# Sixteen query/key projection units moved from the opening stage into the attention rounds of a gated attention-plus-GLU kernel

## The chip, the cores and the metric

The kernel runs on one core of a Trainium2 chip. The metric is the device time of one execution in microseconds (us), lower is better. The engines are TensorE (PE; its weight loads are listed as PEld), VectorE (DVE), ScalarE (ACT), GpSimd (POOL) and SyncE (SP), which here only issues DMAs. POOL and ACT can issue DMAs too.

## The reference

For 2048 tokens of width 448 the program computes two blocks from the same input and mixes them by a gate that depends on the token:

```python
# A: attention, 16 heads of 28
qkv = (x @ wqkv).reshape(B, S, 3, H, 28)          # -> q, k, v
p = softmax(einsum("bhqd,bhkd->bhqk", q, k) * 28 ** -0.5)
a = einsum("bhqk,bhkd->bhqd", p, v) @ wo
# B: gated linear unit, 1792 hidden
gate = x @ W_gate; up = x @ W_up
b = (relu(gate) * up) @ W_down
g = sigmoid((x * gate_w).sum(-1))
out = g * a + (1 - g) * b
```

## The kernel before

**Arithmetic.** Every fp32 operand of a projection is split into a rounded high part and the rest ("low"), and the products that matter are added up. With the width of 448 laid out as three chunks of 128 and one of 64, a projection of one tile takes 11 matmuls (`TERMS`, `NT` = 11). One such group of 11 that fills one PSUM tile of 128x512 is called a unit here.

**Stage 1, the head** (everything ahead of the rounds). Tokens come in four blocks `tb` of 512. Queries and keys together are 896 columns, or `NQ` = 7 column blocks `c` of 128. So there are 28 units `qk(tb, c)` (L424); each result is split into high and low by ACT and DVE and sent by POOL to DRAM (`qk_d`, L435). There are 16 units `vproj(tb, t)` for the values (L442). The first 9 qk units run alone, three more follow, and the rest alternate with the values (`mixed`, L515 to L519). Keys and queries of heads 0, 1 and 2 are loaded back from `qk_d` by SP (`load_k` L164, `load_q` L169) in a layout that stacks the high and low parts on partitions. The first 36 of the row-maximum tiles (`smax`, L190: two matmuls and one DVE reduction) and the first 8 score tiles are mixed into the later units; `first = 9` says from which place of `mixed` on. POOL also writes the split input blocks 1 to 3 to DRAM (`spill_x`, L395), since their room in SBUF is needed.

**Stage 2, 32 rounds.** A round is half a head: 8 of the 16 key blocks against all queries. What each engine does in a round, and in which order, is written out as a string of letters (`ROUNDS`, L46 to L71); the loop at L740 reads it and records the instructions in that order. The letters that matter here:

- `s`: one score tile, two matmuls (L306) and one evacuation by ACT (L310 with the exponential, L312 as a copy); `m`: one maximum tile (L200, L204)
- `x`: one matmul of the gate and up projections (L600). 22 of them, two units, make one hidden block `i`; ACT takes the relu of the gate half (L610), DVE multiplies (L613), SP stores the product
- `w`: split the next gate/up weights into high and low on ACT and POOL (`split_f`, L572)
- `b`, `A`: running minimum over key blocks (L256) and its reduction over partitions on DVE (L263 to L279); `g`: subtract that from 4 tiles on POOL (L285); `e`: exponential of two of the 4 tiles on ACT (L296)
- `P`, `Q`: 32 matmuls each of probabilities times values (L653), 64 a round
- `n`, `N`, `c`, `f`: small steps that end a head; `D`: split a block of W_down; `l`, `u` in the first round finish the last qk unit and load head 2

All engines take their instructions in the written order, and so does SP its DMAs. The rounds hold 1188 `x`, which is 54 of the 56 hidden blocks. The gate itself (`gates`, L553: sigmoid of 16 columns) runs in round 0 through `small_things(1)`.

**Stage 3, the tail.** Two more hidden blocks, the output projection of attention (`wout`), the product with W_down (`down`, L906) and the final mix, in an order written as a list `todo` (L922 to L950).

Of the kernel before, what the change touches and what calls it, by code (L numbers as in the profile page):

```python
# [32 lines left out]
NQ = 2 * D // P  # L33
WARM = 11
# [11 lines left out]
FIRST = "sbbsbAxxxxlusxgxsxxsxssxsxxxsxxsesxxxxbegxxseexwPbbAQ"  # L46

A1 = "smsxxxswbxxxsgbsbnxxxxxssxssxxsAxemxwxmgxsmxxmcessxxxsmxsxbxeggxxxxxesebxeefbewxmmNAwPQ"

Ee = "gswmwsxxxxbsxgsxsxxbebxxxsxxssxxAxssxxemxxxmxsmxeexgmxxsexmxmxxsemxxxsgsbesbbewAwPQ"  # L50

Oe = "sgmgwsxxxxbssxxxsxbxxbxnsxsxsxsAwsxmxxemxxsmxeemsegwxmxxxxmsmxxgexNxsxsbesbxexbcwefxPAQ"

A8 = "wwwsmsxxsxxxxbsxbxgsexxsbxxxxsssxxgxxsAxmxmexxsxemxxgxmsxmexxmsxmxexxgessbbesPewbAQ"

O = "ssbnsxxxxsxbxNxbxxggsxxxxsxxxsxsxxssxxAmxsxxemsxmxexxmxsmxxemmgexsbxxxsbcxxxsbxAxmgeePefeQ"
# [28 lines left out]
def gated_mix_kernel(ctx, tc, x, wq, wo, wgu, wd, out):  # L85
# [49 lines left out]
    x_d = {(tb, r): dram.tile([P, 4 * TB + P], F32, name=f"x_d_{tb}_{r}")[:, :4 * TB].rearrange("p (c t) -> p c t", c=4) for tb in range(1, NB) for r in range(2)}  # L135
# [27 lines left out]

    def load_k(h):  # L164
        k = qk_d[2 * DH * h:2 * DH * h + DH].rearrange("d r t -> (d r) t")
        for a in (0, 2 * DH):
            nc.sync.dma_start(f32(K[h % 3])[a:a + 2 * DH], k)

    def load_q(h):  # L169
        Q[h] = QS[h % 3].rearrange("p j t -> p (j t)")  # L170
        if h > 2:
            nc.sync.dma_start(f32(Q[h])[GD:GD + 2], f32(Q[h])[GD + 2:GD + 4])
        for a in range(2):
            for r in range(2):
                nc.sync.dma_start(f32(Q[h])[2 * DH * a + r:2 * DH * (a + 1):2], qk_d[2 * DH * h + DH:2 * DH * (h + 1), a])
# [112 lines left out]
    def take_exp():  # L288
        q = min(todo_exp, key=lambda q: (q[0], q[2], -q[1]))
        k = halves.pop(q, 0)  # L290
        if k:
            todo_exp.remove(q)
        else:
            halves[q] = 1
        q = QUAD[q][:, 2 * k:2 * k + 2].rearrange("p c t -> p (c t)")
        nc.scalar.activation(q, q, AF.Exp, scale=-SCALE)  # L296
# [35 lines left out]


    with tc.tile_pool(name="qkv", bufs=1) as pa:
        W = pa.tile([P, 7, 2 * D + VC], F32R, name="W")
# [78 lines left out]
        def st_tile(tb, c):  # L414

            k = sent[0]
            sent[0] += 1
            if k < 15 and k % 5 > 2:
                return outs[k % 5 - 3]
            if c == NQ - 1 and tb == 0:  # L420
                return pair[0][:, 2:].bitcast(F32R)
            return pa.tile([P, 2, TB], F32R, name=f"st_{tb}_{c}", tag="st", bufs=3)

        def qk(tb, c, terms=TERMS, among=()):  # L424
            ps = ps_any(f"qk_{tb}_{c}", c == NQ - 1)
# [3 lines left out]
            st = st_tile(tb, c)  # L429

            def send():
                act_high(st[:, 0], ps)
                low(st[:, 1], ps, st[:, 0])
                queue = nc.sync if (tb, c) == (0, NQ - 1) else nc.gpsimd
                queue.dma_start(qk_d[c * P:(c + 1) * P, :, tb * TB:(tb + 1) * TB], f32(st))  # L435


            sends.append(send)
            if (tb, c) != (0, NQ - 1):
                sends.pop()()  # L440

        def vproj(tb, t, among=()):  # L442
            ps = ps_any(f"v_{tb}_{t}", tb == 0 and t > 1)
            for n, (a, b) in enumerate(TERMS):
                nc.tensor.matmul(ps[:, :VC], xf(tb, b)[:, t * P:(t + 1) * P], W[:, a, 2 * D:], start=(n == 0),  # L445
# [46 lines left out]
        w2 = load_w(2)  # L492
# [4 lines left out]
        split_w(*w2)  # L497
# [14 lines left out]
        units = [(qk, 3, 1), (qk, 2, 2), (qk, 3, 2)]  # L512
        units += [(qk, tb, c) for c in range(3, NQ) for tb in range(NB - 1, -1, -1)]
        vs = [(vproj, tb, t) for tb in range(NB - 1, -1, -1) for t in range(4)]
        mixed = units[:2]  # L515
        units = units[2:]
        while units or vs:
            mixed += units[:1] + vs[:1]
            units, vs = units[1:], vs[1:]  # L519
        spills = {15 + 3 * k: (NB - 1 - k // 2, k % 2) for k in range(6)}  # L520
        m, first, ahead = 0, 9, MAXIMA
        for n, (f, *a) in enumerate(mixed):
            if n == 0:
                split_w(*w5)
            if n == 6:
                load_k(1)
                load_q(1)
            if n == 8:
                split_w(*w3)
            if n == 13:  # L530

                nc.gpsimd.memset(f32(K[2])[96:128], -1.0)
            if n == 16:
                load_k(2)
            if n == len(mixed) - 6:
                fetch_f(0)
            if n in spills:
# [23 lines left out]
    fe = ctx.enter_context(tc.tile_pool(name="fe", bufs=1, side="right"))  # L561
# [8 lines left out]
    done = starts[-1] // (2 * NT)  # L570
    assert len(ROUNDS) == 2 * H and starts[-1] % (2 * NT) == 0 and done <= NB * NF, (len(ROUNDS), starts)
# [24 lines left out]

    def gu_mm(ps, i, s, n):

        a, b = (BY_CHUNK if i else HIGH_FIRST)[n]
        nc.tensor.matmul(ps, WS[i][:, s, a], xf(i // NF, b), start=(n == 0), stop=(n == NT - 1))  # L600
# [44 lines left out]
    def pv(v, part):  # L645
# [11 lines left out]
        if v % 2 == 0:  # L657
            OS[h] = fe.tile([P, TB], F32, name=f"os_{h}", tag="os", bufs=2)
# [55 lines left out]
    passes = [(*divmod(k, 2), n) for k in range(2 * done) for n in range(NT)]  # L714
# [3 lines left out]
    def small_things(u):  # L718
# [6 lines left out]
        if u == 1:  # L725
            gates()
# [261 lines left out]
```

## Time and profile before

| quantity | value |
|---|---|
| median of 3 timed runs | 1201.19 us (1199.29 to 1202.57) |
| span of the profiled execution | 1198.9 us |
| PE busy | 1183.7 us, 6183 matmuls |
| DVE, ACT, POOL busy | 902.8, 878.2, 748.9 us |
| head | 0 to 131.3 us |
| rounds 0 to 31 | 131.3 to 1007.4 us |
| tail | 1007.4 to 1198.9 us |

The profiled execution has no time of its own beside its span; the median of the timed runs lies 2.3 us above that span, so much lies around the first and the last instruction or is spread between executions. A round is taken to end when its last probability-times-value matmul has started, and the head when the last value matmul has started. [...]

### The profile page before, as it was taken

How to read it: one execution, taken by the hardware profiler on the slowest of the kernel's cores; microseconds unless marked ns; L12 is line 12 of the kernel's file. 1: busy time of each engine (PE TensorE's matmuls, PEld its weight loads, DVE VectorE, ACT ScalarE, POOL GpSimd, SP SyncE). 2: the span in 40 equal slices, each digit the busy share in tenths (PEclk: the TensorE clock that was granted, in tenths of full speed). 3: DMA queues.
4: the chain of work that ended last, by engine and by line, in shares of the span. 5: the costliest groups of instructions: out<-in, count | busy, mean ns of one | idle time of the engine just before them, and what ended most of it. 6: DMA issues, size and time to landing. Idle time of an engine off the chain costs nothing.

```text
span 1198.9 us, 16948 instructions
## 1 busy us (share of the span) xinstructions
PE 1183.7 (99%) x6183; PEld 820.1 (68%) x6183; DVE 902.8 (75%) x1179; ACT 878.2 (73%) x1082; POOL 748.9 (62%) x326
## 2 busy tenths in 40 slices
PE   9999999999999999999999999999999999999998
PEld 6888755556656666666666666666666666899997
DVE  6466798888898989898888989898988653544242
ACT  5321789999999888888788888888888896422121
POOL 4222387889897777766676767777767786522020
PEclk9999999999999999999999999999999999999999
DMA  9956354354535453443536443436443425743342
GB/s 317 319 207 250 136 191 137 111 141 143 156 129 159 148 163 114 124 122 117 150 119 186 118 129 110 128 117 191 112 126 105 138 89 161 218 136 119 114 128 75
DMA packets 63486, 178.35 MB, mean 149 GB/s; under 512 B 13050, under 2 KB 19650, under 8 KB 58754
## 3 DMA queue, kind: packets, MB, share of 16 engines
q1 hardware_dynamic: 56812, 151.53, 41.1%
q0 software_dynamic: 6160, 25.30, 5.5%
q8 instruction: 48, 0.79, 0.3%
q10 hardware_dynamic: 432, 0.46, 0.1%
q14 instruction: 34, 0.28, 0.1%
HBM read 118.58 MB, written 58.87 MB: 148 GB/s over the span
## 4 chain that ended last, share of the span: by engine, by line
PE 85%; DVE 5%; ACT 3%; DMA 3%; issue 1%; POOL 1%; SPq 1%; DVEq 0%; POOLq 0%; ACTq 0%
PE gu L600 19%; PE s L306 18%; PE po L653 18%; PE sm L200 10%; PE acc L893 10%; PE qk L427 6%; PE wo L852 3%; PE v L445 3%; DVE r L256 1%; ACT P L310 1%; DVE mx L204 1%; ACT P L312 1%; ACT P L296 1%; DMA ls<-os 1%; DMA wor<-wo_d 1%
## 5 line engine op out<-in xcount | busy, mean ns | idle before, releaser
L285 POOL TENSOR_TENSOR P<-P,rm 128x2048 f32<-128x2048 f32 x102 | 470.7, 4633 | 95.5 <-DVE rm L279 79.7
L600 PE MATMUL gu<-X,wg 128*128 128x512 f32 x1232 | 364.6, 395 | 0.7 <-ACT rl L610 0.7
L204 DVE TENSOR_REDUCE mx<-sm 128x1 f32<-128x1024 f32 x256 | 301.5, 1215 | 40.9 <-PE sm L200 40.5
L306 PE MATMUL s<-Q,K 128*128 128x512 f32 x1024 | 316.8, 405 | 6.2 <-ACT V L310 1.9
L600 PEld LDWEIGHTS gu<-X,wg 128*128 128x128 f32 x1232 | 231.2, 188 | 56.7 <-ACT rl L610 2.0
L306 PEld LDWEIGHTS s<-Q,K 128*128 128x128 f32 x1024 | 178.1, 188 | 98.5 <-DVE mn L265 13.4
L312 ACT ACTIVATE P<-s 128x1024 f32<-128x1024 f32 x204 | 202.9, 1031 | 44.2 <-PE s L306 41.6
L653 PE MATMUL po<-P,V 128*32 128x512 f32 x1640 | 227.7, 594 | 0.4 <-ACT P L296 0.4
L296 ACT ACTIVATE P<-P 128x1024 f32<-128x1024 f32 x204 | 213.2, 1072 | 2.1 <-POOL P L285 1.8
L310 ACT ACTIVATE P<-s 128x1024 f32<-128x1024 f32 x206 | 201.5, 1039 | 9.0 <-PE s L306 7.7
L256 DVE SCALAR_TENSOR_TENSOR r<-s,r 128x1024 f32<-128x1024 f32 x124 | 151.6, 1223 | 19.0 <-ACT P L312 10.5
L200 PE MATMUL sm<-K,Q 128*128 128x512 f32 x520 | 163.7, 399 | 0.7 <-DVE mx L204 0.6
L653 PEld LDWEIGHTS po<-P,V 128*32 128x32 f32 x1640 | 63.5, 110 | 116.3 <-issue 108.8
L653 PE MATMUL po<-V 128*32 128x512 f32 x408 | 135.9, 594 | 0.0
L285 POOL TENSOR_TENSOR V<-V,rm 128x2048 f32<-128x2048 f32 x24 | 111.1, 4634 | 23.0 <-DVE rm L279 19.3
L121 ACT ACTIVATE hh<-hr 128x512 fp32r<-128x512 f32 x52 | 32.8, 631 | 117.9 <-PE acc L893 111.8
L200 PEld LDWEIGHTS sm<-K,Q 128*128 128x128 f32 x520 | 91.3, 188 | 33.2 <-ACT P L310 5.6
L127 DVE TENSOR_TENSOR hh<-hr,hh 128x512 fp32r<-128x512 f32 x52 | 47.8, 926 | 82.6 <-ACT hh L121 78.9
L893 PE MATMUL acc<-WD,hh 128*128 128x448 f32 x480 | 100.7, 368 | 0.0
L893 PEld LDWEIGHTS acc<-WD,hh 128*128 128x128 f32 x480 | 90.1, 188 | 8.8
L256 DVE SCALAR_TENSOR_TENSOR r<-s,P 128x1024 f32<-128x1024 f32 x50 | 61.1, 1223 | 38.3 <-ACT P L312 38.3
L271 DVE TRANSPOSE_TENSOR_REDUCE mn<-r 128x32 f32<-128x1024 f32 x63 | 78.0, 1238 | 1.3
(87 smaller groups left out, 1142.6 us busy)
## 6 DMA issues: line engine op xcount, KB each, us to landing
wg<-ws_d SPq DMA_DIRECT2D x42, 896.0 KB
K<-qk_d SPq DMA_DIRECT2D x32, 448.0 KB
Q<-qk_d SPq DMA_DIRECT2D x64, 224.0 KB
h_d<-h SPq DMA_DIRECT2D x56, 256.0 KB
hr<-h_d SPq DMA_DIRECT2D x52, 256.0 KB
ws_d<-wg SPq DMA_DIRECT2D x14, 896.0 KB
qk_d<-st POOLq DMA_DIRECT2D x21, 512.0 KB, 3.2
wgr<-wgu SPq DMA_DIRECT2D x13, 512.0 KB
```

The source lines that it names most:

```text
L200: nc.tensor.matmul(ps[:, c, :], Q[h][:, u * P:(u + 1) * P], K[h % 3][:, k0:k0 + TB], start=True, stop=True)
L204: nc.vector.tensor_reduce(to, ps, axis=AX.XY, op=OP.max)
L256: nc.vector.scalar_tensor_tensor(r, ps, -1.0, before, op0=OP.mult, op1=OP.min)
L271: nc.vector.tensor_reduce(MN[:, 1:3], R2.pop((v, j)).rearrange("p a (b r) -> p a b r", r=32), axis=AX.X, op=OP.min, apply_transpose=True)
L285: nc.gpsimd.tensor_tensor(QUAD[q], QUAD[q], m, op=OP.subtract)
L296: nc.scalar.activation(q, q, AF.Exp, scale=-SCALE)
L306: nc.tensor.matmul(ps[:, c], K[h % 3][:, k * P:(k + 1) * P], Q[h][:, j * TB:(j + 1) * TB], start=True, stop=True)
L310: nc.scalar.activation(dst, ps, AF.Exp, scale=SCALE)
L312: nc.scalar.activation(dst, ps, AF.Copy, scale=-1.0)
L600: nc.tensor.matmul(ps, WS[i][:, s, a], xf(i // NF, b), start=(n == 0), stop=(n == NT - 1))
L653: nc.tensor.matmul(po[32 * j:32 * j + 32], V[:, h // 4 % 2, k, h % 4], AT.pop((v, k, j)), start=(k == k0), stop=(k == k0 + NK // 2 - 1))
L893: nc.tensor.matmul(ACC[i // NF][t][:, :D], HH[i][:, a, t * P:(t + 1) * P], wd_high_low(f, b), start=(f == 0 and n == 0), stop=(f == NF - 1 ...
```

## The change

**Which units move.** Only the column blocks 0, 1 and 2 of queries and keys (`NE` = 3) stay in the head: 12 units, which is all that heads 0 to 4 need. The other four column blocks (`NL` = 4) times four token blocks, 16 units, become the first 176 `x` of the rounds. The gate and up work comes after them in the same stream, so each of its blocks stands 176 `x` later. The strings of letters are new for each round. They hold 1364 `x` in place of 1188, so again 54 hidden blocks are done before the tail. Rounds 0 to 3 hold 44 `x` each (before: 22, 33, 33, 33), rounds 4 to 27 hold 40 or 43 in turn (before 33 up to round 8, then 40 and 37 in turn), the last four 45, 50, 47, 50 (before 37, 47, 41, 44).

```diff
+NE = 3
+NL = NQ - NE
+VO = NE * P
+QP = NL * NB * NT
-E = "gsmsxxxxssebxxbbxxxsxxxxmxAexxssxgsxxsxxsxxmxxsxxemsmexgxexmxxxmsxmxexsbxsgebsebAPQ"
+R12 = "sxxsxxgxxbsxwxbwsbxxxsxxxsxxxssxxAxxswsxgExxmxwmsxxxmxxxsmxsgxxmxxmxxEsbxsgxxsEbebPAmmeQ"
...
+    WB = [fe.tile([P, 7, 2 * P], F32R, name=f"wb_{k}", tag="wg", bufs=2) for k in range(NL // 2)]
...
+    def send_qk(ps, c, tb, queue):
+        high, rest = (fe.tile([P, TB], F32R, name=f"{t}_qk_{c}_{tb}", tag=t, bufs=2) for t in ("rl", "h"))
+        act_high(high, ps)
+        low(rest, ps, high)
+        for r, t in enumerate((high, rest)):
+            queue.dma_start(qk_d[c * P:(c + 1) * P, r, tb * TB:(tb + 1) * TB], f32(t))
...
+    def next_x(tb, n):
+        c = BY_CHUNK[n][1] % 4
+        if n == NT - 1 or BY_CHUNK[n + 1][1] % 4 != c:
+            for r in range(2):
+                nc.sync.dma_start(f32(X[0][r])[:, c], x_d[tb, r][:, c])
+    def qk_mm(ps, u, n):
+        tb, c = divmod(u, NL)
+        a, b = BY_CHUNK[n]
+        nc.tensor.matmul(ps, WB[c // 2][:, a, c % 2 * P:(c % 2 + 1) * P], xf(tb, b), start=(n == 0), stop=(n == NT - 1))
+        if c == NL - 1:
+            next_x((tb + 1) % NB, n)
```

**What goes with it.** The weights of the moved units (`WB`) take the two buffers that the gate/up weights use later; their low parts are made by POOL. The input blocks are needed again in the rounds, so all four of them (8 transfers of 1024 KB in place of 6) go to DRAM, and at the end of each of rounds 0 to 3 the next block is loaded chunk by chunk into the one that is left. The results of the moved units go to DRAM over SP, in two transfers each. In the head every second unit is now sent in two transfers too.

**The head's order.** The three qk units that were followed by qk and v in turn are now followed by the 16 value units alone, and the 36 maximum tiles begin at place 4 of `mixed`:

```diff
-        units = [(qk, 3, 1), (qk, 2, 2), (qk, 3, 2)]
-        units += [(qk, tb, c) for c in range(3, NQ) for tb in range(NB - 1, -1, -1)]
...
-        m, first, ahead = 0, 9, MAXIMA
+        mixed = [(qk, 3, 1), (qk, 2, 2), (qk, 3, 2)]
+        mixed += [(vproj, tb, t) for tb in range(NB - 1, -1, -1) for t in range(4)]
+        spills = {2 + 2 * k: (NB - 1 - k // 2, k % 2) for k in range(2 * NB)}
+        m, first, ahead = 0, 4, MAXIMA
...
-        if u == 1:
-            gates()
...
-    def take_exp():
+    def take_exp(whole):
...
+    before(3, (gates,))
```

On PE, ahead of the first maximum tile (`sm`, which reads the keys `K` and queries `Q` of head 0), there stood before:

```order
L427 MATMUL qk_2_414<-X_3_113,W 128x512 x7
L427 MATMUL qk_2_414<-X_3_114,W 128x512 x4
L445 MATMUL v_0_430<-W,X_3_113 128x450 x7
L445 MATMUL v_0_430<-W,X_3_114 128x450 x4
...
L427 MATMUL qk_3_517<-X_1_117,W 128x512 x7
L427 MATMUL qk_3_517<-X_1_118,W 128x512 x4
L445 MATMUL v_3_532<-W,X_3_113 128x450 x6
L200 MATMUL sm_541<-K_102,Q_105 128x512 x2
```

And at the same place, from the twelfth qk unit to the first maximum tile, there stands now:

```order
L485 MATMUL qk_2_427<-X_3_121,W 128x512 x7
L485 MATMUL qk_2_427<-X_3_122,W 128x512 x4
L500 MATMUL v_0_445<-W,X_3_121 128x450 x7
L500 MATMUL v_0_445<-W,X_3_122 128x450 x4
L500 MATMUL v_1_461<-W,X_3_121 128x450 x4
L255 MATMUL sm_468<-K_104,Q_107 128x512 x2
```

Six units and six matmuls stood between the twelfth qk unit and the first maximum tile; one unit and four matmuls do now.

At the start of round 2, behind the probability-times-value matmuls of round 1, PE had scores (`s`), a maximum tile and the second hidden block's up half (`gu`):

```order
L306 MATMUL s_0_2_1592<-Q_106,K_103 128x512 x2
L200 MATMUL sm_1596<-K_104,Q_1183 128x512 x2
L306 MATMUL s_2_2_1600<-Q_106,K_103 128x512 x2
L600 MATMUL gu_1_1604<-X_111,wg_1284 128x512 x2
L600 MATMUL gu_1_1604<-X_112,wg_1284 128x512
L600 MATMUL gu_1_1604<-X_111,wg_1284 128x512
L306 MATMUL s_4_2_1612<-Q_106,K_103 128x512 x2
L600 MATMUL gu_1_1604<-X_111,wg_1284 128x512
L306 MATMUL s_6_2_1618<-Q_106,K_103 128x512 x2
```

Now the same scores stand there with a projection unit (`qk`, from the weights `wb`) between them:

```order
L361 MATMUL s_0_2_1382<-Q_108,K_105 128x512 x2
L255 MATMUL sm_1386<-K_106,Q_625 128x512 x2
L361 MATMUL s_2_2_1390<-Q_108,K_105 128x512 x2
L669 MATMUL qk_1394<-X_119,wb_113 128x512 x2
L361 MATMUL s_4_2_1398<-Q_108,K_105 128x512 x2
L669 MATMUL qk_1394<-X_120,wb_113 128x512
L669 MATMUL qk_1394<-X_119,wb_113 128x512 x2
L669 MATMUL qk_1394<-X_120,wb_113 128x512
L669 MATMUL qk_1394<-X_119,wb_113 128x512
L361 MATMUL s_6_2_1409<-Q_108,K_105 128x512 x2
```

Between the third and the fourth score tile of the round stand five projection matmuls where one gate/up matmul stood.

**Other edits.** A letter `E` takes the exponential of all four tiles in one instruction where `e` takes two (the other `e` of the pair falls away). `gates` moves from round 0 into the tail, ahead of the fourth `down`. Head 2's keys and queries and the first two gate/up weight blocks are loaded in the head. The packing of column blocks for heads 4 to 15 follows the plain order of the input (`rows_kq`), which changes only row numbers in `qk_d`.

More of the change, by code (lines that the diff above doesn't have):

```diff
@@ L44 @@
 NP = 10
[L46 to L56, printed above, removed]
@@ L133, in gated_mix_kernel @@
     qk_d = dram.tile([2 * D, 2, S + P], F32, name="qk_d")[:, :, :S]
-    x_d = {(tb, r): dram.tile([P, 4 * TB + P], F32, name=f"x_d_{tb}_{r}")[:, :4 * TB].rearrange("p (c t) -> p c t", c=4) for tb in range(1, NB) for r in range(2)}
+    x_d = {(tb, r): dram.tile([P, 4 * TB + P], F32, name=f"x_d_{tb}_{r}")[:, :4 * TB].rearrange("p (c t) -> p c t", c=4) for tb in range(NB) for r in range(2)}
     v_d = {g: dram.tile([P, NK, 4, 32], F32, name=f"v_d_{g}") for g in (2, 3)}
@@ L318, in xf @@
         return X[tb][b // 4][:, b % 4]
-    WR, WS, pair, sends = {}, {}, [], []
+    WR, WS = {}, {}
+    fe = ctx.enter_context(tc.tile_pool(name="fe", bufs=1, side="right"))
+    OX = fe.tile([P, 2, TB], F32, name="ox")
+    WB = [fe.tile([P, 7, 2 * P], F32R, name=f"wb_{k}", tag="wg", bufs=2) for k in range(NL // 2)]
     def fetch_f(i):
@@ L412, in gated_mix_kernel @@
         sent = [0]
[L414 to L422, printed above, removed]
         def qk(tb, c, terms=TERMS, among=()):
-            ps = ps_any(f"qk_{tb}_{c}", c == NQ - 1)
+            ps = ps_any(f"qk_{tb}_{c}")
             for n, (a, b) in enumerate(terms):
@@ L428, in qk @@
                 mix(n, among)
[L429 to L440, printed above, removed]
+            k = sent[0]
+            sent[0] += 1
+            if k % 2:
+                send_qk(ps, c, tb, nc.gpsimd)
+                return
+            st = outs[k // 2 % 2]
+            act_high(st[:, 0], ps)
+            low(st[:, 1], ps, st[:, 0])
+            nc.gpsimd.dma_start(qk_d[c * P:(c + 1) * P, :, tb * TB:(tb + 1) * TB], f32(st))
         def vproj(tb, t, among=()):
@@ L569, in gated_mix_kernel @@
         starts.append(starts[-1] + order.count("x"))
-    done = starts[-1] // (2 * NT)
-    assert len(ROUNDS) == 2 * H and starts[-1] % (2 * NT) == 0 and done <= NB * NF, (len(ROUNDS), starts)
+    done = (starts[-1] - QP) // (2 * NT)
+    assert len(ROUNDS) == 2 * H and (starts[-1] - QP) % (2 * NT) == 0 and done <= NB * NF, (len(ROUNDS), starts)
     def split_f(i, high, low, part=(0, 1)):
@@ L713, in gated_mix_kernel @@
     parts = 0
-    passes = [(*divmod(k, 2), n) for k in range(2 * done) for n in range(NT)]
+    passes = [(*divmod(k, 2), n) for k in range(-NL * NB, 2 * done) for n in range(NT)]
     units = []
@@ L772, in gated_mix_kernel @@
             elif o == "w":
-                ready = -(-starts[v + 2] // NT)
+                ready = -(-max(0, starts[v + 2] - QP) // NT)
                 ready = min(ready + ready % 2, 2 * NF)
-                while parts < ready and (parts < 4 or parts // 2 - 2 in finished):
+                while parts < ready and parts // 2 - 2 in finished:
                     split_f(parts // 2, act_high, pool_low, (parts % 2,))
```

161 lines of the change are left out of this document (95 added, 66 removed).

## The prediction

> **What bounds the kernel now.** I read the page's busy times first, then the chain of work that ended last, then the busy times of each engine by stage.
>
> ```profile
> PE 1183.7 (99%) x6183; PEld 820.1 (68%) x6183; DVE 902.8 (75%) x1179; ACT 878.2 (73%) x1082; POOL 748.9 (62%) x326
> PE 85%; DVE 5%; ACT 3%; DMA 3%; issue 1%; POOL 1%; SPq 1%; DVEq 0%; POOLq 0%; ACTq 0%
> ```
>
> PE is listed as busy nearly all the time and carries 85% of the chain, so work that only changes its place on PE changes nothing by itself. But listed matmuls overlap, and short waits vanish in such a sum. So I price a matmul by the distance between starts, from the timeline of a quiet stretch and from the longest pieces of the chain:
>
> ```profile
> 602.19 1.33 PE L600 MATMUL gu<-X,wg 128*128 128x512 f32 x5
> 603.35 0.64 PE L306 MATMUL s<-Q,K 128*128 128x512 f32 x2
> 592.23 7.00 PE po L653 x64
> ```
>
> Five matmuls in 603.35 - 602.19 = 1.16 us make 0.232 us each; a round's 64 probability-times-value matmuls take 7.00 us. With these two prices I compare need and time by stage (the columns: stretch, length, then busy time and count for PE, PEld, DVE, ACT, POOL, the clock, the DMA share and GB/s):
>
> ```profile
> 0.00:38.30 38.30, 36.47 (x144) 26.12 (x145) 23.64 (x38) 21.00 (x38) 17.28 (x29) 1.00 0.90 312
> 38.30:131.30 93.00, 92.71 (x422) 78.90 (x421) 53.86 (x57) 23.99 (x56) 19.24 (x29) 1.00 0.62 233
> 131.30:186.50 55.20, 51.88 (x277) 30.47 (x275) 49.05 (x60) 49.79 (x66) 40.28 (x23) 1.00 0.48 161
> 186.50:241.70 55.20, 54.29 (x295) 32.98 (x291) 48.39 (x64) 51.45 (x63) 48.16 (x23) 1.00 0.44 136
> 241.70:351.00 109.30, 108.21 (x588) 65.86 (x582) 98.24 (x129) 102.70 (x126) 95.78 (x43) 1.00 0.44 138
> 351.00:377.80 26.80, 26.69 (x149) 16.64 (x145) 23.90 (x30) 24.43 (x28) 20.77 (x7) 1.00 0.56 168
> 377.80:902.90 525.10, 525.08 (x2876) 335.74 (x2871) 465.04 (x618) 459.79 (x519) 382.08 (x119) 1.00 0.45 134
> 902.90:1007.40 104.50, 102.24 (x568) 66.04 (x562) 64.99 (x95) 94.27 (x109) 81.63 (x26) 1.00 0.33 109
> 1007.40:1198.90 191.50, 186.11 (x900) 167.37 (x892) 75.71 (x94) 50.74 (x79) 43.72 (x33) 1.00 0.46 141
> ```
>
> The strings give the matmuls of each stage (one per x, two per s and m). Rounds 4 to 7, the fifth row: 132 + 128 + 64 = 324 at 0.232, and four blocks of 7.00, make 103.2 of 109.3 us, so PE stood 6.1 us. In the same way: rounds 0 and 1 (146 matmuls with what is left of the head) 47.9 of 55.2, 7.3 lost; rounds 2 and 3 51.6, 3.6 lost; round 8 25.8, 1.0 lost; rounds 9 to 27 (1645) 514.6, 10.5 lost, 0.55 a round; rounds 28 to 31 (305) 98.8, 5.7 lost. Together 34.2 us are lost in the rounds. That is all that the rounds can give. Rounds with splits of weights (`w`) and 33 x lose 1.0 to 1.8 each from round 2 on, later ones 0.55. What ends the waits there, in rounds 4 to 7:
>
> ```profile
> PEld s L306 <- ACT P L310: 2.8, 9, 0.6
> PEld s L306 <- DVE mn L265: 2.5, 3, 0.8
> PEld s L306 <- DVE r L256: 2.4, 6, 0.5
> PEld gu L600 <- ACT rl L610: 1.4, 2, 0.7
> ```
>
> PE waits for a PSUM tile that ACT or DVE has not emptied, a few tenths at a time. ACT is busy 102.7 of 109.3 us there, and has the splits to do as well. In the head and the tail PE needs nearly all of the time, while ACT works 24 of 93 us and 51 of 191.5.
>
> **What leaves the head.** The head's timeline on PE:
>
> ```profile
> 1.20 4.10 PE L472 MATMUL warm_ps<-warm 128*128 128x512 bf16 x11 [1.20 <-DVE warm L469]
> ...
> 38.26 2.40 PE L445 MATMUL v<-W,X 128*128 128x450 f32 x11
> 40.50 2.69 PE L427 MATMUL qk<-X,W 128*128 128x512 f32 x11
> 43.03 2.42 PE L445 MATMUL v<-W,X 128*128 128x450 f32 x11
> ...
> 53.83 0.63 PE L200 MATMUL sm<-K,Q 128*128 128x512 f32 x2
> ```
>
> A unit takes 43.03 - 40.50 = 2.53 us, a value matmul (40.50 - 38.26) / 11 = 0.204. Sixteen units fewer: **-40.5 us**.
>
> **What the head gains as a wait.** The first maximum tile stood at 53.83, six units behind the twelfth qk unit. Now it comes after one value unit and four matmuls: 40.50 + 4 x 0.204 = 41.3 us. It needs head 0's keys and queries. When do they land? The queue of SP, its waits from 35 to 60 us, and what the two DMA queues moved from 35.8 to 48.6 us:
>
> ```profile
> 35.87 0.82 SPq L167 DMA_DIRECT2D K<-qk_d  x2
> 36.73 3.38 SPq L175 DMA_DIRECT2D Q<-qk_d  x4
> ...
> 46.20 0.72 SPq L175 DMA_DIRECT2D Q<-qk_d  x1
> SPq L175 <- DMA Q<-qk_d: 0.7, 2, 0.4
> q1 hardware_dynamic: 788, 2.53, 62.1%
> q0 software_dynamic: 401, 1.50, 33.0%
> ```
>
> The loads of head 0 are issued from 35.87 on, and nothing in the change makes that earlier: they wait for the ninth unit's results, as before. The two last issues for head 1 were themselves held until an older query load had landed, the very last one at 46.20; each load of head 0 has a semaphore that a later one uses again. So the second of the four query loads landed at about 46.2, and at about 1.1 us apart (the issue before it stood about that much earlier) the fourth lands at 48.4. The bounds: head 0's six loads are 2 x 448 + 4 x 224 = 1792 KB (1.84 MB); at q1's 2.53 MB in 12.8 us in order of issue they would be there at 35.87 + 9.3 = 45.2; and 53.83 at the latest, since no wait for them is shown. So PE stands from 41.3 to 48.4: **+7.1 us** (3.9 to 12.5). All of PE queues up behind it: the values, then the maxima.
>
> After such a stop PE may also start slowly. The one start from rest that the trace has is the first row above: 11 matmuls of 512 columns from 1.20 to 5.36 (the next start), 0.378 each in place of 0.232, 1.6 us in all. The granted clock is 1.00 in every stage row, so the trace shows no second case. I take **+1.6 us** (0 to 1.6). [...] The 4.10 us row agrees with a slow start; that a pause within a run does it is shown by no trace here.
>
> The other edits of the head cost nothing by this trace: DVE has 36 maxima to reduce in 15 units now, but works 53.86 of 93 us; the eight input copies (1024 KB each) are issued by POOL, busy 19.24 of 93, behind the qk results; the DMA share of 0.62 leaves room.
>
> **What the rounds take in.** 1364 - 1188 = 176 matmuls at 0.232: **+40.8 us** if nothing of it fills a wait. The evacuations come along, and the displaced gate/up work takes its own with it to later rounds. Rows for these, for the exponential and for `gates`:
>
> ```profile
> L127 DVE TENSOR_TENSOR st<-qk,st 128x512 fp32r<-128x512 f32 x21 | 14.3, 683 | 10.7 <-ACT st L121 10.7
> L613 DVE TENSOR_TENSOR h<-gu,rl 128x512 f32<-128x512 f32 x56 | 38.2, 681 | 11.8 <-PE gu L600 5.9 <-ACT rl L610 5.9
> L121 ACT ACTIVATE st<-qk 128x512 fp32r<-128x512 f32 x21 | 12.5, 594 | 34.9 <-PE qk L427 34.9
> L296 ACT ACTIVATE P<-P 128x1024 f32<-128x1024 f32 x204 | 213.2, 1072 | 2.1 <-POOL P L285 1.8
> L130 POOL TENSOR_TENSOR wg<-wgr,wg 128x384 fp32r<-128x384 f32 x26 | 25.8, 1012 | 23.8 <-ACT wg L121 21.9 <-POOL mn L636 1.6
> L556 DVE TENSOR_SCALAR e<-e 128x16 f32<-128x16 f32 x1 | 4.3, 4305 | 0.0
> L558 DVE TENSOR_SCALAR gate<-gate 128x16 f32<-128x16 f32 x1 | 4.3, 4251 | 0.0
> ```
>
> In rounds 0 to 3, 16 units with one DVE step each (16 x 0.683 = 10.9 us) replace 5.5 hidden blocks (5.5 x 0.681 = 3.7), 7.2 us more for DVE; against that `gates` leaves it, 8.6 us of round 0. ACT and POOL are rid of the splits there until round 3. In the tail `gates` lies on a DVE that works 75.71 of 191.5 us: 0 (if it held one `down` back as in round 0, 8.6).
>
> **What the rounds give back.** A round now holds 40 to 44 x. PE's need rises to 28.3 us with 44 x (92 x 0.232 + 7.00) and to 27.4 and 28.1 with 40 and 43, while rounds 4 to 7 took 27.3 with their splits. So the longest engine's need is now PE's, and waits for ACT and DVE, whose work per round hardly grows, have more matmuls standing between them. What stays lost, by my choice between the 0.55 that rounds without splits lose now and what rounds with them lose: rounds 0 and 1 2.8 (from 7.3; `gates` gone, no splits), 2 and 3 1.4 (3.6), 4 to 11 6.0 at 0.75 (8.7: splits stay, spread out), 12 to 27 6.4 at 0.40 (8.8), 28 to 31 3.2 (5.7). Together 19.8 of 34.1, given back: **-14.3 us**. The 57 whole exponentials help: two of 512 cost 2 x 594 ns and one of 1024 1072, a fixed part of about 0.1 us, some 6 us of ACT in all, which is not on the path by itself. Bounds: nothing is given back, or all rounds get to 0.35 (11.2 lost), 23 given back.
>
> Reloading the input at the end of rounds 0 to 3 is costed at nothing: the reload of a chunk starts when three of 11 matmuls of the last unit are done, and the round's 7.00 us block stands before the next unit. Without that cover it would cost some us each time.
>
> Sum: -40.5 + 40.8 + 7.1 + 1.6 - 14.3 = -5.3 on the profiled span, and the same on the median of the runs: 1201.2 - 5.3 = 1195.9, I say **1196**.
>
> **The rivals.**
>
> *The rounds take the units at full price.* The waits listed hang on DVE and ACT steps in a fixed order; if a score tile still comes as early after its predecessor as before, x elsewhere does not shorten the wait, and only `gates` and the whole exponentials give something, about 1. Then 1201.2 + 0.3 + 8.7 - 1 = 1209, slower. For it: rounds 9 to 27 lose 0.55 already with ACT at 459.8 of 525.1, so the waits are not one of capacity. Against it: rounds with fewer x lose three times that. It decides when the rounds give back less than 5.4. Chance 0.20.
>
> *Head and rounds cancel out.* The stop at the first maximum is 7 to 9, the rounds give 6 to 12: 1198 to 1204, about 1201. Chance 0.19.
>
> *The stop is short.* Head 0's loads land at 45.2 (POOL's queue yields to SP's), PE does not slow down, and the rounds lose 0.40 each (12.8, so 21.3 given back): 1201.2 + 0.3 + 3.9 - 21.3 = 1184. For it: q1 had only 62.1% of the engines. Against it: the 46.20 row. Chance 0.21.
>
> My forecast has the other 0.40. That the change doesn't do what it says, with the units waiting in the rounds for the reloaded input, would show as PE waiting for a DMA; it belongs to the first rival.
>
> **How the numbers follow.** A measurement of this kernel tells about 0.3% (3.6 us) from no change. Faster by more: forecast and third rival, 0.61; within: 0.19; slower: 0.20. The range reaches from the third rival's side (1182 with 23 given back and 3.9 lost, and a little beyond, since the 0.35 is my choice: 1180) to 1209.
>
> **What would show it.** Right: the value stage's first maximum at about 48 with PE idle 7 us before it, waiting for a load of Q; the last value matmul near 102 (131.3 less 15 units of 2.53 and plus 8.7: 102.0); rounds 4 to 7 lasting about 28.5 each; the tail as long as before. Wrong: a first maximum that starts at 42; rounds 12 to 27 that lose over 0.6 each; a PE wait for X at the seam of rounds 0 to 3.

## The result, and the profile after

The changed kernel takes 1207.38 us (median of 4 runs, 1206.96 to 1207.83) against 1201.12 us (4 runs, 1199.29 to 1202.57): ratio 1.0062, 95% interval 1.0046 to 1.0078. It is slower by 6.3 us, where 5.3 faster was forecast. The profiled run took 1207.77 us with a span of 1206.0, so 1.8 us lie around it (before: 2.3). That is near enough to compare by spans: 1206.0 - 1198.9 = +7.1 us.

The busy times, the shares of the chain and the granted clock on the page:

```profile
PE 1184.7 (98%) x6183; PEld 825.1 (68%) x6183; DVE 899.1 (75%) x1171; ACT 881.2 (73%) x1023; POOL 746.6 (62%) x325
PEclk9899999999999999999999999999999999999999
PE 86%; DMA 4%; DVE 3%; ACT 3%; issue 1%; SPq 1%; POOL 1%; DVEq 0%; ACTq 0%; POOLq 0%
```

PE does the same 6183 matmuls. ACT has 59 instructions fewer (57 of them by exponentials that were two halves and are one). On the chain DVE fell from 5% to 3% and DMA rose from 3% to 4%. Which DMAs, the list of PE's waits says (total, times, longest):

```profile
PE sm L255 <- DMA Q<-qk_d: 8.1, 1, 8.1
PE gu L661 <- DMA X<-x_d: 3.2, 2, 2.0
PE wo L914 <- POOL on L177: 2.9, 1, 2.9
```

The last of these is old (1.8 us before, and 1.5 to 3.5 in the profiles below: a reason to compare times, and not spans, where 2 us matter). The other two are new. The busy times by stage, cut at the head's end, after rounds 1, 3, 7, 11, 27 and 31:

```profile
0.00:38.30 38.30, 36.79 (x143) 26.80 (x144) 22.31 (x34) 20.15 (x34) 19.19 (x35) 1.00 0.90 304
38.30:105.40 67.10, 59.00 (x263) 50.11 (x262) 43.15 (x38) 18.95 (x45) 14.81 (x24) 0.92 0.77 273
105.40:157.50 52.10, 52.10 (x289) 33.99 (x292) 42.59 (x60) 44.85 (x51) 30.51 (x11) 1.00 0.49 166
157.50:215.70 58.20, 58.20 (x317) 38.00 (x313) 51.77 (x69) 52.16 (x59) 40.87 (x14) 1.00 0.63 204
215.70:330.70 115.00, 114.49 (x623) 72.71 (x615) 98.62 (x128) 105.68 (x122) 100.30 (x48) 1.00 0.52 159
330.70:445.30 114.60, 114.23 (x619) 72.86 (x615) 97.54 (x128) 102.78 (x117) 95.16 (x43) 1.00 0.54 169
445.30:905.80 460.50, 456.89 (x2470) 293.34 (x2466) 400.08 (x526) 390.65 (x416) 320.05 (x98) 1.00 0.44 133
905.80:1014.80 109.00, 108.36 (x591) 68.62 (x585) 65.47 (x96) 95.50 (x102) 81.84 (x27) 1.00 0.36 115
1014.80:1206.00 191.20, 184.61 (x900) 168.62 (x892) 77.55 (x98) 50.50 (x80) 43.88 (x33) 0.99 0.46 142
```

The head ends at 105.4 (131.3 before, 102 forecast), the rounds take 909.4 us (876.1), the tail 191.2 (191.5): -25.9 + 33.3 - 0.3 = +7.1. In the head PE is busy 59.0 of 67.1 us, and the clock column falls to 0.92.

To see the rounds I price every matmul of a round by its start distance in dense stretches of both kernels (0.231 us, and 0.1075 for one of the 64 probability-times-value matmuls) and call the rest of the round lost. These prices are a little lower than the prediction's, so the loss of before is 40.4 us and not 34.2; the differences count.

| rounds | lost before | lost after | given back | forecast |
|---|---|---|---|---|
| 0 to 3 | 11.6 | 2.8 | 8.8 | 6.7 |
| 4 to 11 | 10.6 | 9.5 | 1.1 | 2.7 |
| 12 to 27 | 11.7 | 18.9 | -7.2 | 2.4 |
| 28 to 31 | 6.5 | 5.7 | 0.8 | 2.5 |
| all | 40.4 | 36.9 | 3.5 | 14.3 |

So the first rounds did what was forecast, and rounds 12 to 27 lose more than before. Two of them stand out: round 18 loses 2.5 and round 26 loses 3.8, where most of the others lose about 0.85 (round 25 loses 1.6). The 3.2 us that PE waits for `X` lie in these two.

**The head.** PE's and SP's timelines (start, length, operation, idle time before it):

```profile
38.34 3.23 PE L500 MATMUL v<-W,X 128*128 128x450 f32 x15
49.68 1.19 PE L255 MATMUL sm<-K,Q 128*128 128x512 f32 x2 [8.10 <-DMA Q<-qk_d]
```

```profile
36.37 0.79 SPq L221 DMA_DIRECT2D K<-qk_d  x2
37.20 3.45 SPq L230 DMA_DIRECT2D Q<-qk_d  x4
40.70 1.10 SPq L221 DMA_DIRECT2D K<-qk_d  x2
42.51 4.97 SPq L230 DMA_DIRECT2D Q<-qk_d  x4
48.06 0.61 SPq L403 DMA_DIRECT2D wr<-wq  x1
```

The loads of head 0 are issued where they were, and the first maximum waits for the last of them, from 41.6 to 49.7. The two matmuls of that maximum are then listed at 1.19 us, where the first pair of before took 0.63. The last SP row will matter too: one load of weights of the moved units, issued behind 12 key and query loads of two heads.

**The seams.** The gate/up work goes through the four input blocks in turn, and at three places the next block is loaded over the last one, 8 transfers of 256 KB by SP. Before, these lay in rounds 9, 17 and 25. With 176 matmuls ahead of the stream they lie in rounds 11, 18 and 26. Even rounds also carry the next head's key and query loads on the same queue. SP in round 18, and at the start of round 26:

```profile
629.39 1.71 SPq L742 DMA_DIRECT2D rb<-l_d  x4
631.20 0.84 SPq L656 DMA_DIRECT2D X<-x_d  x2
632.09 0.65 SPq L226 DMA_DIRECT2D Q<-Q  x1
632.79 3.15 SPq L230 DMA_DIRECT2D Q<-qk_d  x4
636.04 4.03 SPq L656 DMA_DIRECT2D X<-x_d  x6
...
846.47 0.92 SPq L221 DMA_DIRECT2D K<-qk_d  x2
848.65 5.91 SPq L656 DMA_DIRECT2D X<-x_d  x8
```

In round 18 five query transfers stand between the second and the third load of `X`; in round 26 the key loads go ahead of all eight. PE then stands:

```profile
851.92 0.72 PE L361 MATMUL s<-Q,K 128*128 128x512 f32 x2
854.65 0.73 PE L661 MATMUL gu<-X,wg 128*128 128x512 f32 x2 [2.01 <-DMA X<-x_d]
```

### The profile page after: what moved, and what is told of

It is laid out like the page before. It is cut to its first block, busy times and chain, and to the rows that moved or that the text cites. A ratio compares the mean times of both kernels' runs of the same rounds, so it can differ in the third digit from the quotient of the medians.

```text
span 1206.0 us, 16979 instructions
## 1 busy us (share of the span) xinstructions
PE 1184.7 (98%) x6183; PEld 825.1 (68%) x6183; DVE 899.1 (75%) x1171; ACT 881.2 (73%) x1023; POOL 746.6 (62%) x325
## 4 chain that ended last, share of the span: by engine, by line
PE 86%; DMA 4%; DVE 3%; ACT 3%; issue 1%; SPq 1%; POOL 1%; DVEq 0%; ACTq 0%; POOLq 0%
PE gu L661 21%; PE po L720 19%; PE s L361 18%; PE sm L255 10%; PE acc L955 9%; PE qk L669 3%; PE wo L914 3%; PE v L500 3%; DVE r L311 2%; ACT P L367 1%; DMA X<-x_d 1%; DMA Q<-qk_d 1%; DMA or<-o_d 1%; ACT P L365 1%; DMA wor<-wo_d 1%
## 5 line engine op out<-in xcount | busy, mean ns | idle before, releaser
L259 DVE TENSOR_REDUCE mx<-sm 128x1 f32<-128x1024 f32 x256 | 306.1, 1217 | 62.5 <-PE sm L255 61.2
L361 PEld LDWEIGHTS s<-Q,K 128*128 128x128 f32 x1024 | 182.6, 188 | 80.5 <-DVE r L311 12.5
L720 PE MATMUL po<-P,V 128*32 128x512 f32 x1640 | 230.6, 595 | 0.0
L351 ACT ACTIVATE P<-P 128x1024 f32<-128x1024 f32 (+1 forms) x158 | 202.6, 1312 | 0.9 <-POOL P L340 0.5
L255 PEld LDWEIGHTS sm<-K,Q 128*128 128x128 f32 x520 | 94.3, 189 | 40.9 <-POOL K L578 8.5
```

What stands on the lines that cost most here:

```text
L255: nc.tensor.matmul(ps[:, c, :], Q[h][:, u * P:(u + 1) * P], K[h % 3][:, k0:k0 + TB], start=True, stop=True)
L259: nc.vector.tensor_reduce(to, ps, axis=AX.XY, op=OP.max)
L361: nc.tensor.matmul(ps[:, c], K[h % 3][:, k * P:(k + 1) * P], Q[h][:, j * TB:(j + 1) * TB], start=True, stop=True)
L720: nc.tensor.matmul(po[32 * j:32 * j + 32], V[:, h // 4 % 2, k, h % 4], AT.pop((v, k, j)), start=(k == k0), stop=(k == k0 + NK // 2 - 1))
```

## The experiments

All ratios are to the kernel before, run on the same chip; the changed kernel stands at 1.0062.

**1. Later maxima (e1_later_maxima).** The maxima begin at place 8 of the mixed units, so the value units cover the landing of head 0's loads.

```diff
-        m, first, ahead = 0, 4, MAXIMA
+        m, first, ahead = 0, 8, MAXIMA
-EARLY = (5, 4, 4, 3, 2, 2, 1, 1)
+EARLY = (3, 3, 2, 2, 2, 1, 1, 1)
```

> The changed kernel with the 36 maximum tiles of the head begun at place 8 of the value stage in place of 4, and the 8 early scores moved back to the last three places. Theory A (the stop at the first maximum, 8.1 us of wait and about 2.3 us of slow clock behind it, is a cost of its own): the first maximum starts at about 50 us without a wait, the clock stays at 1.00, the head ends near 95 to 96 in place of 105.4, and the time is 1197 to 1199. Rival B (the maxima are paced by DVE anyway, 36 x 1.13 us = 41 us from the first one on, and PE then waits for PSUM tiles among them): the head ends at 99 or later and the time is 1202 or more.

Measured: 1.0087 (1.0070 to 1.0103), not faster at all. The wait at the first maximum is gone; another stop begins 7 us behind it. PE, then ACT:

```profile
50.11 0.62 PE L255 MATMUL sm<-K,Q 128*128 128x512 f32 x2
...
56.93 0.63 PE L255 MATMUL sm<-K,Q 128*128 128x512 f32 x2
64.98 1.49 PE L500 MATMUL v<-W,X 128*128 128x450 f32 x3 [7.42 <-ACT zt L505]
```

```profile
63.21 1.23 ACT L168 ACTIVATE wb<-wr 128x576 fp32r<-128x576 f32 x4 [17.46 <-DMA wr<-wq]
64.34 0.52 ACT L504 ACTIVATE V<-v 128x448 f32<-128x448 f32 x1
```

ACT stood 17.46 us at the split of one group of the moved units' weights (`wb`), whose load is the SP row at 48.06 above (47.33 in this run): issued behind the key and query loads of heads 0 and 1, it landed 16 us later. The emptying of the value tiles stands behind that split in ACT's written order, so it waited as well (it went on at 64.34), and PE stood 7.42 us until ACT had emptied a tile. The head ends at 107.2. That is rival B's number without its reason, and neither theory had this: the head has a second gate, which the first stop had hidden.

**2. The second gate too (e5_later_split).** The same, and the split of that group six places later (place 12 in place of 6).

> The later maxima (place 8, early scores at the last three places) and, with them, the split of the third weight block (W2) at place 12 of the value stage in place of 6. The later maxima alone did not help: PE then stood from 57.4 to 65.0 us for a PSUM tile that ACT had not emptied. Theory A (ACT stood in its order at the split of W2, whose load lies on SP's queue behind the keys and queries of heads 0 and 1, and the value evacuations stood behind it; the head has two gates on the same queue): both stops go, the clock stays up, the head ends near 95 to 97, the ratio to the kernel before falls from 1.009 to 0.997 to 1.000. Rival B (the maxima are paced by DVE): the head ends at 99 or later, ratio above 1.002.

Measured: 1.0000 (0.9990 to 1.0011). The head ends at 97.5, with the clock at 1.00 all through it. The two stops together are worth 0.0062 of 1200, 7.4 us by the times, and 7.9 by the head's end.

**3. What the slow clock costs (e3_filler).** 28 needless bf16 matmuls into an unused tile keep PE busy in the wait, of which 1.0 us is left.

```diff
+            if n == 4:
+                idle = ps_w("idle")
+                for _ in range(28):
+                    nc.tensor.matmul(idle[:, 0], warm[:, :P], warm, start=True, stop=True)
```

> The changed kernel with 28 needless bf16 matmuls of 512 columns on PE ahead of the first maximum tile, so that PE works through most of the wait and waits only at its end; the output is not touched by them. Theory A (idleness puts PE at half clock until 54.4 us): the clock record shows no half-clock stretch near 44 to 54, the wait for the queries stays, and the time falls by 2 to 2.5, about 1205. Rival B (the slow stretch has another reason, or what it costs is hidden by DVE's reductions): no change, within 0.7.

Measured: 1.0058 (1.0046 to 1.0071); the time does not tell it from the changed kernel. The trace does. The granted clock (third column from the end) in the changed kernel and, below, with the filler:

```profile
38.30:44.10 5.80, 3.28 (x16) 2.64 (x14) 0.69 (x1) 1.21 (x3) 1.64 (x4) 1.00 0.99 295
44.20:54.30 10.10, 4.62 (x12) 3.96 (x13) 2.26 (x2) 0.00 (x0) 2.28 (x2) 0.50 0.95 352
54.40:60.00 5.60, 5.60 (x27) 4.92 (x27) 4.35 (x5) 1.20 (x4) 0.00 (x0) 1.00 0.89 347
```

```profile
47.00:51.00 4.00, 3.01 (x15) 2.38 (x14) 1.69 (x2) 0.00 (x0) 2.29 (x2) 1.00 0.96 387
51.00:55.00 4.00, 4.00 (x21) 3.54 (x20) 3.34 (x4) 1.21 (x4) 0.00 (x0) 1.00 0.93 320
```

From the first maximum to the head's end it takes 53.5 us with the filler (48.51 to 102.05) and 55.7 in the changed kernel (49.68 to 105.43): the half clock costs 2.2 us. In the six other profiles with this head (e2, e4, e6, e7, e10, e13) the same stretch is 55.0 to 56.3, so 1.5 to 2.8. It is shown by the trace alone. In this profile round 26 lost 4.9 us in place of 3.8 and the tail was 0.8 us longer, which takes most of it back; whether the other runs did the same is not known.

**4. The seams (e2_seam, e6_seam2).** The next head's key and query loads go to other places of rounds 18 and 26: behind the `X` loads in round 26, and in round 18 ahead of them in e2, the queries behind them in e6.

```diff
-                if ns in (1, 9) and v % 2 == 0:
-                    loads(v // 2, load_k if ns == 1 else load_q)
+                at = {18: (1, 4), 26: (8, 12)}.get(v, (1, 9))
+                if ns in at and v % 2 == 0:
+                    loads(v // 2, load_k if ns == at[0] else load_q)
```

> The changed kernel with the loads of keys and queries moved away from the two places where the input block in SBUF is exchanged: in round 18 the query load stands at the 4th score tile in place of the 9th, in round 26 keys and queries at the 8th and 12th in place of the 1st and 9th. Theory A (the 3.8 us in which PE waits for X there come from the key and query loads that stand ahead of the X loads on SP's queue, since the shift by 176 x brought the seams into even rounds): both waits go, time lower by 3 to 4, 1203.5 to 1204.5. Rival B (the X loads themselves, 2 MB, take that long): the waits stay, lower by less than 1.

Measured: 1.0043 (1.0031 to 1.0055). That is theory A's time, but by luck: round 26 fell from 3.8 to 2.0, and round 18 rose from 2.5 to 5.7, so that the rounds together got 0.8 us longer. The profiled run is shorter by 1.4 us in the head and 1.6 in the tail, which the edit does not touch. SP's rows and its waits in round 18:

```profile
633.08 1.71 SPq L742 DMA_DIRECT2D rb<-l_d  x4
634.88 4.67 SPq L656 DMA_DIRECT2D X<-x_d  x8
...
SPq L742 <- DMA l_d<-rq: 6.3, 1, 6.3
```

The small store `l_d`, now issued behind the early query loads, landed late; SP stood 6.3 us for it ahead of `rb` (1.1 in the changed kernel), and the `X` loads queue behind that. So for round 18 the queries go behind the `X` loads: `18: (1, 14)`.

> The second try at the seams: in round 26 as before (keys and queries at the 8th and 12th score tile), in round 18 the keys stay at the 1st and the queries go to the 14th, behind the seam. In the first try round 26 lost 1.8 us less, but round 18 lost 3 us more: the earlier query load lay ahead of the row sums' way through DRAM, for which SP waited, and the X loads stood behind that wait. Theory A (what stands ahead of the X loads on SP and on its queue decides): round 18 loses about 1, round 26 about 2, in all 3 to 3.5 us less than the changed kernel, ratio about 1.003. Rival B (the X loads' own length): round 18 loses 2.5 or more again.

Measured: 1.0033 (1.0018 to 1.0049). Round 18 is at 1.1 and round 26 at 2.0, as theory A had it. By the records this is worth 3.2 us. By the times it is 0.0029, 3.5 us, but by the intervals of the two ratios that can be anything from about 1 to 6. The profile is of the shortest of e6's twelve runs (1199.8 to 1208.8): its span lies 7.9 us under the changed kernel's, and only 3.7 of that in the rounds.

**5. The gates (e4_gates_back, e8_before_gates).** `gates` put back into round 0 of the changed kernel; and the kernel before with `gates` in its tail.

> The changed kernel with the gate computation back in round 0, where it was before (8.6 us on DVE there). Theory A (part of the 6.7 us that rounds 0 and 1 gave back is due to its move): rounds 0 and 1 lose 2 to 4 us more and the time rises by as much, 1209 to 1211. Rival B (the x that stand in these rounds cover it): within 0.7 of 1207.4.

> The kernel before with one edit of the change alone: the gate computation moved from round 0 to the tail. Theory A (it held up round 0, but putting it back into the changed kernel cost only 0.6, since other work covers it): faster by 1 to 3 us, because rounds 0 and 1 have few x to cover it. Rival B (round 0 waits for other things anyway): within 0.7 of the kernel before.

Measured: 1.0067 (1.0055 to 1.0080) and 1.0003 (0.9990 to 1.0016). Neither can be told from its parent. In the trace the gates cost round 0 of the changed kernel 1.7 us, and the kernel before still loses 3.8 in round 0 without them. So the gates' leaving is not what rounds 0 to 3 gained from. Two things are left: the 44 projection matmuls in each, and the weight splits, which left rounds 1 and 2 (four `w` each before, none now). No run separates these. Round 3 keeps its four `w` and lost 0.8 in place of 1.9, which speaks for the matmuls, or for its new order.

**6. Old orders (e7_old_orders, e10_phase).** Rounds 12 to 27 with the strings of before (37 and 40 x in place of 40 and 43; two hidden blocks more go to the tail). In e7 the strings are put in as they are, with four x spread over odd rounds. In e10 five x more stand at the end of round 11, so that the units begin at the same places in the strings as in the kernel before.

> The changed kernel with the orders of rounds 12 to 27 as they were before (37 and 40 x a round in place of 40 and 43, four x put in besides, so that whole blocks come out); two hidden blocks go to the tail, where PE works at full price. Theory A (the waits in these rounds stand at fixed places behind DVE and ACT steps, three more x a round do not shorten them, and the new orders lose more than the old ones): rounds 12 to 27 lose 11 to 13 us in place of 18.9, the time falls by 3 to 7, ratio 1.000 to 1.004. Rival B (the x are cover, as the prediction had it): the rounds lose more with fewer x, 20 or above, and the ratio is 1.007 or more.

Measured: 1.0332 (1.0312 to 1.0351). These are rival B's numbers, but not its reason: rounds 12 to 27 lost 44 us, and PE's waits (of the whole run) show what a place in a string also decides.

```profile
PE gu L661 <- ACT rl L677: 8.4, 4, 2.3
PE gu L661 <- DVE mh L174: 7.2, 4, 2.3
```

A unit of 11 matmuls ends where the eleventh x stands, and then ACT and DVE have to empty it. At the start of round 12 a block of 22 `x` has 2 behind it, where it had 7 in the kernel before. With the added `x` the shift shrinks from five places there to one from round 20 on. Even with one place, rounds 21, 23 and 25 lose 3.2 to 3.5 (before: 0.7 to 1.2). So the strings are written for a phase: those ends now fall beside other work of ACT and DVE.

> The old orders in rounds 12 to 27 once more, now with five x put at the end of round 11 and one taken from round 27, so that each unit begins at the same letter of the string as it did in the kernel before (7 of 22 at the start of round 12; in the failed try it was at 20 after four more x were spread). Two hidden blocks are done in the tail. In the failed try these rounds lost 42 us, most of it waits of the x for a PSUM tile behind the relu or behind the end of a head's maxima. Theory A (an order fits only the place at which units begin and end in it; with the old place the old loss comes back): rounds 12 to 27 lose 11 to 13 us in place of 18.9, no wait for X, ratio 1.000 to 1.002. Rival B (the changed kernel's rounds carry something else that slows the old orders): they lose 18 or more.

Measured: 1.0125 (1.0105 to 1.0144). Rounds 13 to 18 and 20 to 26 lose 0.5 to 0.9, on average 0.72, just as before; thirteen of the changed kernel's rounds 12 to 27 (all but 18, 25 and 26) lose 0.85. But rounds 19 and 27 lose 6.4 and 8.3: the seam now ends at the eleventh `x` of a string that had it at the 22nd before, and another head's stores stand between its loads. The tail, with two hidden blocks more, also waits 5.6 us for gate/up weights.

```profile
644.68 1.82 SPq L656 DMA_DIRECT2D X<-x_d  x4
646.60 1.66 SPq L748 DMA_DIRECT2D o_d<-ox  x4
648.36 2.33 SPq L656 DMA_DIRECT2D X<-x_d  x4
```

So with the old orders and three `x` fewer a round the loss is 0.13 less, not more. Order and number of `x` change together here, so this doesn't show what more `x` alone would do; it shows that 40 and 43 `x`, in the orders as written, did not shorten the waits. What PE's weight loads waited for in rounds 12 to 27 before, and in the changed kernel:

```profile
PEld s L306 <- DVE mn L265: 6.7, 8, 0.8
PEld s L306 <- DVE rm L279: 3.4, 4, 0.8
PEld s L306 <- DVE r L256: 2.7, 12, 0.5
```

```profile
PEld s L361 <- DVE r L311: 5.7, 19, 0.6
PEld gu L661 <- DMA X<-x_d: 4.1, 2, 2.4
PEld s L361 <- DVE mx L259: 3.5, 5, 0.8
```

The waits moved from the partition minimum (`mn`, `rm`) to the running one (`r`) and the maxima (`mx`), and the wait for `X` came on top; the loss in a round did not shrink.

**7. Combinations (e11_head_and_phase, e12_early_unit).** e10 with the repaired head; and the same with unit `qk(3, 0)`, the last that head 0 needs, two units earlier, its loads with it, and maxima from place 6.

> The head's repair and the old orders at their old place together. Theory A: ratio 0.992 to 0.996 (1.000 less some 6 us). Rival B (the tail's two blocks more cost what the rounds win): 0.998 to 1.001.

> As the one before, with the unit of token block 3 and column block 0 moved ahead of three others, so that head 0's keys and queries are loaded 5 us earlier, and the maxima begun at place 6 (early scores at the last four places). Theory A (the loads set when the maxima can begin, and the maxima are the longest work of DVE in the head): no wait at the first maximum, head ends near 95 in place of 97.5, 1 to 2 us less than without it. Rival B (the head is held by PE's own work by then): within 0.7.

Measured: 1.0094 (1.0074 to 1.0115), which is neither theory's, and 1.0086 (1.0066 to 1.0105), not to be told from it, as rival B had it. The seams of e10 stay (7.0 and 8.3 in e11); the early unit moved the head's end from 97.3 to 97.1.

**8. All repairs (e9_head_and_seam, e15_rep_early).** The later maxima and split of experiment 2 with the loads of e6; and that with the early unit.

> The changed kernel with both repairs: later maxima with the later split of W2 (alone: ratio 1.000), and the key and query loads of rounds 18 and 26 moved behind the seams (alone: 1.0033). Theory A (the two costs are separate): they add up, ratio 0.996 to 0.998. Rival B (what is saved in the head is lost again at the later places): 0.999 to 1.001.

> The repaired kernel with the last unit that head 0 needs done one place earlier, head 0's loads issued with it, and the maxima from place 6 of the mixed units rather than 8. Theory A: the head is now held by its matmuls alone, so it ends at 97.5 as in the repaired kernel and the ratio stays within 0.0007 of 0.9988. Rival B: earlier maxima spare DVE a pile-up at the head's end and round 0; then 1 to 2 us faster, ratio 0.997 to 0.998.

Measured: 0.9988 (0.9974 to 1.0001) and 0.9979 (0.9969 to 0.9989). The first can't be told from the kernel before, and lies between its two theories. By the records the two savings do add up: the head ends at 97.7 (e5: 97.5) and the rounds take 905.7 us (e6: the same). But the tail takes 194.7 us (e6: 189.0). PE's work in it is the same in every run but e7 and e10 to e12, and yet it lasts from 189.0 to 195.3 us: PE's wait for `on` differs (1.5 to 3.5 us), half clock followed the longer ones (none behind 1.8 us in the kernel before, 3.4 us of it behind 2.9 in the changed kernel, 6.8 behind 3.5 in e15), and the `acc` matmuls start 0.203 us apart in some stretches and 0.207 in others (12 of them in 2.44 us from 1089.81 on in the changed kernel, in 2.48 from 1046.93 on in the kernel before). What sets that distance is open. The second, 1197.24 us, beats it by about 2.5 us and is the best of all; its head ends at 96.6 (97.7 in e9). That is rival B's number, but the two intervals overlap, and in experiment 7 the same step moved the head by 0.2: whether the early unit adds anything stays open.

**9. Whole or half exponentials (e13_halves, e14_rep_halves).** Each `E` written as `ee`, in the changed kernel and in e9.

> The changed kernel with each of the 57 whole exponentials (E, four tiles in one instruction) written as two halves (ee, two tiles each), all else as changed. Theory A: the whole exponential only saves ACT's fixed part of about 0.1 us each, 6 us in all, off the path; then the time stays within 1 us of the changed kernel, ratio to before 1.0055 to 1.0070. Rival B: an instruction of 2 us holds up ACT's next emptying of a PSUM tile that PE waits for, and is part of the loss in the rounds; then halves are faster by 2 to 4 us, ratio about 1.003, and rounds 4 to 27 lose less each.

> The repaired kernel (later maxima, later split of the second value weights, and key/query loads moved in rounds 18 and 26, measured at ratio 0.9988) with each whole exponential written as two halves. Theory A: within 1 us of the repaired kernel, ratio 0.998 to 1.000. Rival B: faster by 2 to 4 us, ratio about 0.996, clearly under before.

Measured: 1.0051 (1.0037 to 1.0064), beside 1.0062, and 0.9992 (0.9980 to 1.0004), beside 0.9988. Theory A holds for both as far as the intervals go: the whole exponentials are neither the gain nor the loss. Rounds 4 to 27 lose 28.2 us in e13 and 28.4 in the changed kernel.

## Why the prediction was wrong, step by step

**The head's -40.5: right.** One of the 16 units had lain in round 0 (+2.5), and six score and maximum matmuls now lie ahead of the head's end (+1.4), so 36.6 us earlier was due without stops. In e5 it ends 33.8 us earlier; in e15 34.7. What is missing in e5 lies where PE's weight loads wait for DVE's maximum reductions (4.3 us in 12 waits ahead of maxima, 0.7 us in all before), a cost that the prediction put at nothing.

**The stop, +7.1: right in kind, 1 short.** PE waited 8.1 us for the last query load of head 0 (41.6 to 49.7; 7.0 to 8.2 over the profiles with this head).

**The slow clock, +1.6: right in kind, measured 2.2** (1.5 to 2.8). The prediction took the price of the one start from rest in its trace; the half clock in fact lasted through 4.7 us of work.

**What the prediction did not see in the head** is that the stop had a second one behind it (experiment 1). It changed nothing in the sum, since the first hid it, but it is why moving the maxima alone does not help.

**The rounds take in +40.8: right.** With the 17 matmuls that left round 0 taken off, the rounds' need grew by 159 x 0.231 = 36.7 us; their length grew by 33.3.

**The rounds give back -14.3: this is the step that failed; they gave 3.5.** The prediction put it so: waits "have more matmuls standing between them", and chose 0.40 a round for rounds 12 to 27. That came out for rounds 0 to 3 (8.8 given back, 6.7 forecast), where a string had 22 to 33 `x`, though the splits left some of these rounds too (experiment 5). It failed by 9.6 us in rounds 12 to 27. About 4.6 of it are the seams: rounds 18 and 26 above the usual 0.85, of which e6 won back 3.2 by the records. The rest is the choice of 0.40 itself (about 0.6 by the prices used here, which are lower: 88 x 0.001 + 64 x 0.0019 = 0.21 a round): the waits stayed, and the loss rose from 0.72 to 0.85 in a round. There the first rival fits better: e7 shows that the loss hangs on how the order of ACT's and DVE's steps meets the ends of units. Which steps hold it at 0.85 was not tested. Why round 25 loses 1.6 is not settled.

**Input reload at the end of rounds 0 to 3 at nothing: right**; PE's list has no such wait. But the prediction looked only at these four reloads, which are new, and not at the three old ones that the new units shift. A displaced step takes its DMAs to a place with other DMAs. That was in the code: loads of keys and queries in even rounds only, and seams in odd ones.

**Gates, whole exponentials, tail at nothing: right** (experiments 5 and 9; the tail is 0.3 us shorter in the two profiles, less than it differs from run to run).

The miss by the profiled span is 12.4 us: 3.4 in the head's end (105.4 for 102.0: the landing 1.3, the clock 0.6, the rest the matmuls that moved ahead) and 9.3 in the rounds (10.8 of give-back, less those matmuls), less 0.3 in the tail. The range held the time, and it came out nearest to the first rival (1209). That is in part luck: the rival had no seams, and without their 4.6 us the rounds would have given back 8.1, more than the 5.4 up to which it decides. Its reason is half of the truth: it was wrong for rounds 0 to 3, and fits rounds 12 to 27.

## What to carry to other kernels

Work that is moved out of a stage takes away cover: ask of every load there what hides it now, and after the first wait look for the next one behind it, on the same DMA queue and in the written order of each engine (in e1 ACT stood 17.46 us at one split, with the value tiles behind it). Work put into a hand-written order shifts all that follows, so look at the steps that come once in many rounds (here a 2 MB exchange of input) and what shares their queue at the new place. And small waits that sit at fixed steps of other engines need not shrink because more work stands in the round: most of rounds 12 to 27 lost no less than before with three more `x`, while rounds 0 to 3, with 44 `x` in place of 22 to 33, lost less.

## What the runs showed of the hardware

The half clock cost 2.2 us (experiment 3) where the prediction took 1.6. With 8.1 us without matmuls the granted clock of the changed kernel was 0.50 from 44.2 to 54.3: it fell 2.6 us after PE's last matmul, and came back 4.7 us after work began again. At the same place a stop of 7.1 us (e2, e6) or 7.2 (e4) brought 6.8 us at half clock, and one of 8.1 (the changed kernel) or 8.2 (e13) brought 10.2.

Shorter waits did it too. In the tail, PE's wait for `on` was followed by no half clock in the kernel before, where it lasted 1.8 us, by 3.4 us of it in the changed kernel, where it lasted 2.9, and by 6.8 in e15, where it lasted 3.5 (there the clock is 0.83 on average from 1040 to 1060, which makes 6.8 us at 0.50).

A small vector step took as long as POOL's large one beside it. The second `tensor_scalar` of the gates, 128 x 16, took 4.48 us in e4, beside POOL's step, and 0.79 in the tail of the changed kernel. DVE's timeline and POOL's in e4, and the changed kernel's row:

```profile
113.24 4.48 DVE L613 TENSOR_SCALAR gate<-gate 128x16 f32<-128x16 f32 x1
```

```profile
113.09 9.19 POOL L340 TENSOR_TENSOR P<-P,rm 128x2048 f32<-128x2048 f32 x2 [5.63 <-PE qk L669]
```

```profile
L613 DVE TENSOR_SCALAR gate<-gate 128x16 f32<-128x16 f32 x1 | 0.8, 793 | 0.0
```

In e4 it ended at 117.72, when the first of POOL's two steps (9.19 / 2 = 4.6 us each) did. The first `tensor_scalar`, 0.13 us long, had ended at 112.91, before POOL began; the reciprocal between the two took 0.25 us. In the kernel before, where both lie beside POOL's steps, they took 4.30 and 4.25. What made them that long was not tested.
